# Loading v once per token and starting the first batch by other queues, in a chunked attention kernel with a ReGLU feed-forward

## The chip, the core and the metric

The kernel runs on one core of one Trainium2 chip. The engines that matter are TensorE (PE in the profile; PEld is its weight load), VectorE (DVE), ScalarE (ACT), GpSimd (POOL) and SyncE (SP). Transfers between HBM and SBUF are issued by POOL (queue q0 in the profile), SP (q1) or ACT (q10) and all run on the core's 16 DMA engines. The metric is the time of one execution in device microseconds. Three runs of the kernel before gave 247.49, 248.11 and 249.26 us; the median is 248.11.

## What is computed

Four batches, eight heads, 768 tokens, head size 64. Each chunk of 32 queries attends to 8 memory keys of its head, 16 keys to the left of the chunk, its own 32 and 8 to the right: 64 keys in all, fewer at the two ends of the sequence. The result, with the heads side by side, is a 3072 x 512 matrix that goes through a gated feed-forward of width 1536.

```python
for c in range(nc):                                  # chunk = 32, left 16, right 8
    k_full = concatenate([mem_k, k[:, :, l_start:r_end]], axis=2)
    v_full = concatenate([mem_v, v[:, :, l_start:r_end]], axis=2)
    scores = scale * matmul(q_c, k_full.T)
    a = exp(scores - max(scores)); a = a / (sum(a) + 1e-09)
    out[:, :, chunk c] = matmul(a, v_full)
x = out.transpose(0, 2, 1, 3).reshape(B * S, H * D)
result = (maximum(x @ w_gate, 0) * (x @ w_val)) @ w_out
```

All inputs and the result are float32 in HBM. The kernel computes in 16-bit types and accumulates in float32.

## The kernel before

**Tiles and blocks.** A tile is 128 tokens of one batch (four chunks, all eight heads). There are 24 tiles, six to a batch, numbered through. The feed-forward works on blocks of two or four tiles (`BLOCKS = [2, 2, 2, 4, 4, 4, 4, 2]`), so blocks 0 and 1 are tiles 0 to 3.

**One tile's attention.** q and k are brought to a layout with the head dimension on partitions (TensorE transposes, L225 for the first batch, L264 later, DMA transposes for the last six tiles). `scores` (L298) makes the 128 x 512 scores of a tile in 32 small matmuls. Then a chain over VectorE and ScalarE: row maximum (L311), subtraction (L318), exponential in three pieces (L326), row sum (L330), reciprocal (L334), normalisation (L341). `p_t` transposes the probabilities (L347), a copy takes them to SBUF, `values` multiplies them with v, and a copy gives the tile's columns of `xT`, the feed-forward's input.

**v in slots.** From batch 1 on, v lies in `v_bd`, two buffers used in turn. For every pair of heads and every chunk, the buffer holds a block of 128 partitions by 128 columns: 64 rows for the first head's keys in the left 64 columns, 64 for the second head's in the right 64, zeros elsewhere. Rows 0 to 55 of each half are the 56 tokens of the chunk's context, rows 56 to 63 the memory values. Since neighbouring chunks overlap, one load of 56 rows per chunk (`load_v_rows`, L173, two per batch: one for each half) brings most tokens twice. The zeros are written by POOL (L129), the memory values are copied into all 24 chunks of a pair of heads by eight small transfers per batch (`mem_rows`, L156; 8 partitions by 24 pieces of 128 bytes each), by SP for batch 1 and by POOL for batches 2 and 3. With this layout one matmul per chunk and pair of heads gives the tile's values (L377, 16 per tile).

**v in the first batch.** Here v is loaded tile by tile as it lies in HBM (`load_v_tile`, six transfers), and TensorE shifts it into chunk windows by multiplying with slices of a band matrix (`shift`, L204, 68 matmuls in all), with a copy by ScalarE or VectorE behind each of twelve groups. `values` then needs four matmuls for the memory values (L363) and 32 half-height ones for the rest (L370) per tile.

**q and k in the first batch.** They are loaded by POOL in three pairs of tiles (L216; k and q, 256 KB each in SBUF, converted to bfloat16 on the way) and transposed in 96 small TensorE transposes (L225).

**Feed-forward.** `first` (L396) multiplies the block's `xT` with 128 columns of `w_gate` or `w_val` at a time, four matmuls for each; ScalarE takes the rectified gate out (L402), VectorE multiplies it with the other half (L408). `second` (L421) multiplies with `w_out`, ScalarE takes the result out and stores it. The weights are loaded by POOL in four groups of columns (`load_gate_val`, L109), and blocks 0 and 1 are worked off in turn, group by group, since the weights are still on their way.

**What sets the order.** The kernel lists all operations with durations that it assumes, what they depend on, and priorities. `schedule()` runs through assumed time and picks, for each engine, the first ready operation; the result is a fixed order of instructions on each engine. On the chip each engine follows this order, and an instruction whose inputs are late holds up everything behind it on its engine. POOL's order (the loads) is written out by hand. [...]

Of the kernel before, what the change touches and what calls it, by code (L numbers as in the profile page):

```python
# [19 lines left out]
def kernel(  # L20
# [12 lines left out]
    nc = tc.nc  # L33
# [19 lines left out]
    BAND0 = 48  # L53

    LATE_QK, LATE_P = 18, 18

# [25 lines left out]

    band = const.tile([128, BAND0 + 176], F16, name="band")
    ident_h = band[:, BAND0:BAND0 + 128]
# [12 lines left out]
    v_q = v_bd[0][:, 0:2].rearrange("p h c d -> p (h c d)").rearrange("p (h c d) -> p h c d", h=HP, d=D)  # L97
    v_n = {}
    qk_p = {(i, r): const.tile([128, H, 2 * D], BF16, name=f"qk_p_{i}_{r}") for i in range(2) for r in range(TPB // 2)}
# [15 lines left out]
    def make_band():  # L115
        nc.gpsimd.memset(band, 0.0)
        nc.gpsimd.affine_select(
            out=band, in_=band, compare_op=ALU.not_equal, fill=1.0, base=BAND0,
            pattern=[[-1, BAND0 + 176]], channel_multiplier=1)
# [8 lines left out]
    def zero(eng, t, hp):  # L128
        eng.memset(t[:, hp].rearrange("p c d -> p (c d)").bitcast(F32), 0.0)  # L129


    def mem_load():
        for par in range(2):
            nc.sync.dma_start(
                kmem_f[:, par, :],
                bass.AP(tensor=mem_k.tensor, offset=mem_k[0, par, 0, 0].offset,
                        ap=[[2 * NMEM * D, B * HP], [D, NMEM], [1, D]]),
            )
# [13 lines left out]
    def mem_rows(eng, b, n):  # L152
        hp, par = divmod(n, 2)
        p = slice(64 * par + CTX, 64 * par + CTX + NMEM)
        src = vmem[p, b, HP * par + hp]
        eng.dma_start(  # L156
            v_bd[b % NSET][p, hp, :, D * par:D * par + D],
            bass.AP(tensor=src.tensor, offset=src.offset,
                    ap=[src.ap[0], [0, NCH], [1, D]]))
# [18 lines left out]
    def v_parts(b, par, c0, c1):  # L178
        parts = []
        if (b, par, c1) == (B - 1, 1, HP * NCH):  # L180
            c1 -= 1
            parts.append((b, par, 0, 48, c1, c1 + 1))
        return parts + [(b, par, 0, CTX, c0, c1)]


    def load_v_tile(t):
        v_n[t] = ldpool.tile([128, H, D], F16, tag="qk_b", name="v_n")
        nc.gpsimd.dma_start(
            v_n[t],
            bass.AP(tensor=v.tensor, offset=v[0, 0, 128 * t, 0].offset,  # L190
                    ap=[[D, 128], [S * D, H], [1, D]]))

    def shift(c0):
        ps = TMP["sh", c0] = fps.tile([128, 2, HP, D], F32, tag="fps", name="vs_ps")
        for i in range(2):
            t, g = divmod(c0 + i, 4)
            parts = [(t, BAND0 + CH * g - 16)]
            if g == 0 and t:
                parts.append((t - 1, BAND0 + 112))
            if g == 3 and t < TPB - 1:  # L200
                parts.append((t + 1, BAND0 - 48))
            for n, (src, x) in enumerate(parts):
                for par in range(2):
                    nc.tensor.matmul(ps[D * par:D * par + D, i], lhsT=band[:, x:x + 64],  # L204
                                     rhs=v_n[src][:, HP * par:HP * par + HP, :],
                                     start=(n == 0), stop=(n == len(parts) - 1))

    def shift_copy(c0, eng):
        copy(eng, v_q[:, :, c0:c0 + 2, :].rearrange("p h c d -> p c h d"), TMP.pop(("sh", c0)))

# [37 lines left out]
    def new_batch(b):  # L248
        qT[b] = kvpool.tile([128, HP, S], BF16, name="qT")
        kT[b] = kvpool.tile([128, HP, NCH, KW], BF16, name="kT")  # L250
        src = kmemT[:, b]
        nc.vector.tensor_copy(
            kT[b][:, :, :, 16:16 + NMEM],
            bass.AP(tensor=src.tensor, offset=src.offset,
                    ap=[src.ap[0], [NMEM, HP], [0, NCH], [1, NMEM]]))
# [101 lines left out]
    def values(a):  # L357
# [3 lines left out]
        if b == 0:  # L361
            for hp in range(HP):
                nc.tensor.matmul(ps[:, hp, :], lhsT=vmem_0[:, hp, :], rhs=x[:, hp, :],  # L363
                                 start=(hp == 0), stop=False, skip_group_check=True)
            for hp in range(HP):
                for g in range(4):
                    r = slice(CH * g, CH * g + CH)
                    for par in range(2):
                        p = D * par
                        nc.tensor.matmul(ps[p:p + D, hp, r], lhsT=v_q[p:p + CTX, hp, 4 * t + g, :],  # L370
                                         rhs=x[p:p + CTX, hp, r], start=False, stop=(hp, g) == (HP - 1, 3),
                                         skip_group_check=True)
            return
# [83 lines left out]
    op("warm", {"DVE": 0.15}, lambda e: nc.vector.memset(warm, 0.0), prio=(-9,))  # L457
    op("warm2", {"ACT": 1.5}, lambda e: nc.scalar.activation(warm, warm, ACT.Exp), ["warm"], prio=(-9,))
    op("vmem_f", {"DVE": 0.55}, lambda e: nc.vector.memset(vmem_f, 0.0), prio=(-8,), after=["warm"])
    op("kml", {"SP": 1.4}, lambda e: mem_load(), prio=(-9,))  # L460
    op("vml", {"SP": 1.4}, lambda e: pattern_load(), ["vmem_f"], prio=(-8,), after=["kml"])
    op("if", {"DVE": 0.25}, lambda e: nc.vector.tensor_copy(ident_f, ident_h), ["ident"], prio=(-7,))
    op("ib", {"DVE": 0.25}, lambda e: nc.vector.tensor_copy(ident_b, ident_h), ["ident"], prio=(-6.9,))
    op("kmt", {"PE": 0.25}, lambda e: mem_keys_t(), [("kml", 1.8), "if"], prio=(-5,), take=["aps"])
    op("kmc", {"ACT": 0.35}, lambda e: nc.scalar.copy(kmemT.rearrange("p b h m -> p (b h m)"), TMP.pop("kmem")),
       ["kmt"], prio=(-5,), give=["aps"])
    op("vm0", {"DVE": 0.5}, lambda e: nc.vector.tensor_copy(vmem_0, vmem_f), [("vml", 1.8)], prio=(-3,))
    for b in range(B):
        op(("new", b), {"DVE": 0.4}, lambda e, b=b: new_batch(b), ["kmc"], take=["kv"],
           prio=(-4.5,) if b == 0 else (1, TPB * b - 2, 0), after=[("t", TPB * b - 2, 0)] if b else [])  # L470
# [31 lines left out]
    for a in range(NT):  # L502
        b, t = divmod(a, TPB)
        last = t == TPB - 1
        for i in (1, 0):
            if b == 0:
# [7 lines left out]
            if a >= LATE_QK:  # L514
# [8 lines left out]
               (1, a - i, 0), ["aps"], ["qk"], pace(max(a - i, 0)))  # L523
            op(("tc", a, i), psum16(HP * 128), lambda e, a=a, i=i: qk_copy(a, i, engine[e]), [("t", a, i)],
               (1, a - i, 0), (), ["aps"])
        op(("s", a), {"PE": 0.36}, lambda e, a=a: scores(a),
           [(("t", a, 0), LAND) if a >= LATE_QK else ("tc", a, 0), ("tc", a, 1)]
           + ([] if last else [("tc", a + 1, 1)] if b or t % 2 == 0 else [("tc", a + 1, 1), ("tc", a + 2, 1)])
           + ([("tc", a ^ 1, 0)] if b == 0 else []), (1, a, 1), ["sps"],
# [14 lines left out]
        if b == 0:  # L544
            for c0 in (4 * t, 4 * t + 2):
                need = {c // 4 for c in (c0, c0 + 1)} | {max(c0 - 1, 0) // 4, min(c0 + 2, NCH - 1) // 4}
                gone = ([t - 1] if c0 % 4 == 0 and t else []) + ([t] if c0 == NCH - 2 else [])
                op(("sh", c0), {"PE": 0.4}, lambda e, c0=c0: shift(c0), [("vn", n) for n in sorted(need)] + ["ident"],
                   (1, a, 7.5), ["fps"], ["qk"] * len(gone), [("s", t)])
                op(("shc", c0), psum(2 * HP * D), lambda e, c0=c0: shift_copy(c0, engine[e]), [("sh", c0)],  # L550
                   (1, a, 7.6), (), ["fps"])
        blk = block_of[a]
        j = a - starts[blk]
        op(("v", a), {"PE": 0.45 if b else 1.0}, lambda e, a=a: values(a),
# [64 lines left out]
    for t in range(3):  # L619
        load_v_nat(t)  # L620
# [170 lines left out]
```

## Time and profile before

| | |
|---|---|
| three runs, median | 248.11 us (247.49 to 249.26) |
| the profiled execution, its own time | 247.81 us |
| its span, first to last instruction | 246.0 us |
| PE busy | 233.3 us, 95% |
| DVE, ACT, POOL busy | 132.7, 117.6, 90.6 us |
| PE busy in 0 to 15, 15 to 20, 20 to 25 us | 7.37, 3.84, 4.89 us |
| first feed-forward matmul | 22.24 us |
| queue q0 (POOL) | 94368 packets, 16.42 MB |
| queue q1 (SP) | 11760 packets, 2.64 MB |

Busy times are sums over instructions on an engine. PE's busy time says that matmuls were under way, not that they ran at their best rate, so the start-to-start distance of groups in the timeline is used for prices. Times within the span count from its start. The time of an execution is 1.8 us longer than its span.

### The profile page before, as it was taken

What the parts mean: (1) busy time and instruction counts of PE and PEld (TensorE: products, weight loads), DVE (VectorE), ACT (ScalarE), POOL (GpSimd) and SP (SyncE); (2) the same over time, 40 slices, a digit from 0 to 9 for tenths busy, and PEclk for the clock granted to TensorE, in tenths of its full rate; (3) what the DMA queues carried; (4) which work ended last, traced back from release to release, by engine and by line L of the source; (5) the groups of instructions that cost most, each with busy time, mean ns of one, the idle gap of its engine ahead of it and who ended that gap; (6) DMA issues with size and microseconds to landing.
All of it is one profiled execution on the core that took longest, in us unless ns stands there. A gap on an engine that the chain in (4) does not pass through costs nothing.

```text
span 246.0 us, 6397 instructions
## 1 busy us (share of the span) xinstructions
PE 233.3 (95%) x2673; PEld 139.8 (57%) x2673; DVE 132.7 (54%) x260; ACT 117.6 (48%) x265; POOL 90.6 (37%) x105
## 2 busy tenths in 40 slices
PE   0869999999999999999999999999999999999994
PEld 0646887884488645555445545555445444444873
DVE  2372757984139748796048779999342034320430
ACT  2755867753275445643245575765332232312432
POOL 8965799813268991099921050000000000000000
PEclk9999999999999999999999999999999999999999
DMA  7999999999999899999999999671101210002102
GB/s 74 173 179 203 203 96 119 174 175 127 133 223 154 80 102 136 75 75 147 179 192 158 67 76 109 130 147 25 23 0 45 85 44 0 0 35 95 43 3 85
DMA packets 109757, 25.76 MB, mean 105 GB/s; under 512 B 100769, under 2 KB 106657, under 8 KB 109729
## 3 DMA queue, kind: packets, MB, share of 16 engines
q0 software_dynamic: 94368, 16.42, 107.7%
q1 hardware_dynamic: 11760, 2.64, 8.9%
q10 hardware_dynamic: 3600, 6.29, 7.9%
q8 instruction: 21, 0.34, 0.6%
q14 instruction: 8, 0.06, 0.1%
HBM read 32.06 MB, written 6.29 MB: 156 GB/s over the span
## 4 chain that ended last, share of the span: by engine, by line
PE 92%; DMA 2%; DVE 2%; issue 1%; ACT 1%; POOL 1%; ACTq 0%; POOLq 0%
PE v_ps L396 26%; PE g_ps L396 26%; PE out_ps L421 25%; PE xT_ps L377 3%; PE s_ps L298 3%; PE qk_ps L264 2%; DMA qk_p<-in_k_dram 2%; PE pT_ps L347 2%; PE xT_ps L370 2%; PE vs_ps L204 1%; PE qk_ps L225 1%; PE xT_ps L363 1%; DVE mx L311 1%; POOL qk_p L216 1%; DVE dif L318 1%
## 5 line engine op out<-in xcount | busy, mean ns | idle before, releaser
L408 DVE TENSOR_TENSOR gvT<-v_ps,g_relu 128x256 f16<-128x256 f32 (+1 forms) x96 | 53.0, 555 | 56.7 <-PE v_ps L396 41.0
L396 PE MATMUL g_ps<-xT,w_gate_sb 128*128 128x256 f16 (+1 forms) x384 | 78.5, 327 | 0.0
L396 PE MATMUL v_ps<-xT,w_val_sb 128*128 128x256 f16 (+1 forms) x384 | 78.2, 326 | 0.0
L402 ACT ACTIVATE g_relu<-g_ps 128x256 f16<-128x256 f32 (+1 forms) x96 | 46.9, 489 | 50.7 <-PE g_ps L396 50.0
L421 PE MATMUL out_ps<-w_out_sb,gvT 128*128 128x512 f16 (+2 forms) x300 | 65.7, 371 | 0.0
L396 PEld LDWEIGHTS <-w_gate_sb 128*128 128x128 f16 x384 | 36.4, 98 | 24.0 <-issue 0.4
L396 PEld LDWEIGHTS <-w_val_sb 128*128 128x128 f16 x384 | 35.9, 98 | 20.9 <-issue 0.2
L421 PEld LDWEIGHTS <-gvT 128*128 128x128 f16 x300 | 28.0, 98 | 29.9
L78 ACT COPY o_sb<-out_ps 128x512 f32<-128x512 f32 (+2 forms) x25 | 14.2, 567 | 37.2 <-PE out_ps L421 28.2
L326 ACT ACTIVATE p_exp<-dif 128x256 f16<-128x256 f32 (+2 forms) x72 | 19.5, 336 | 9.0 <-DVE dif L318 8.8
L243 POOL DMA_DIRECT2D qk_b<-in_k_dram x18 | 16.5, 915 | 15.0 <-issue 8.4
L311 DVE TENSOR_REDUCE mx<-s_ps 128x8 f32<-128x512 f32 x24 | 16.5, 688 | 8.3 <-PE s_ps L298 8.0
L156 POOL DMA_DIRECT2D v_bd<-vmem x16 | 10.1, 642 | 27.7 <-DMA v_bd<-in_v_dram 27.7
L330 DVE TENSOR_REDUCE sm<-p_exp 128x8 f32<-128x512 f16 x24 | 16.4, 682 | 6.0 <-ACT p_exp L326 5.9
L78 ACT CAST xT<-xT_ps 128x512 f16<-128x512 f32 x19 | 11.1, 584 | 15.4 <-PE xT_ps L377 10.2
L243 POOL DMA_DIRECT2D qk_b<-in_q_dram x18 | 16.4, 913 | 3.1 <-issue 2.0
L341 DVE TENSOR_TENSOR p_n<-p_exp,rinv 128x512 f16<-128x512 f16 x24 | 16.5, 687 | 0.4
L318 DVE TENSOR_TENSOR dif<-s_ps,mx 128x512 f32<-128x512 f32 x24 | 16.4, 684 | 0.4
L173 POOL DMA_DIRECT2D v_bd<-in_v_dram x7 | 14.0, 2015 | 1.0 <-POOL v_bd L129 0.6
L377 PEld LDWEIGHTS <-v_bd 128*128 128x128 f16 x288 | 9.6, 96 | 4.7 <-issue 1.1
L78 ACT COPY kT<-qk_ps 128x512 bf16<-128x512 bf16 x17 | 10.8, 641 | 2.9 <-PE qk_ps L225 1.9
L129 POOL MEMSET v_bd<- 128x1536 f32 x8 | 10.7, 1397 | 0.0
(52 smaller groups left out, 156.8 us busy)
## 6 DMA issues: line engine op xcount, KB each, us to landing
out_dram<-o_sb ACTq DMA_DIRECT2D x23, 256.0 KB
v_bd<-in_v_dram POOLq DMA_DIRECT2D x5, 672.0 KB, 17.6
qk_b<-in_k_dram POOLq DMA_DIRECT2D x18, 128.0 KB, 6.1
qk_b<-in_q_dram POOLq DMA_DIRECT2D x18, 128.0 KB, 6.4
w_out_sb<-in_moe_w_out_dram POOLq DMA_DIRECT2D x2, 768.0 KB, 11.2
qk_p<-in_k_dram POOLq DMA_DIRECT2D x3, 256.0 KB, 5.2
qk_p<-in_q_dram POOLq DMA_DIRECT2D x3, 256.0 KB, 7.1
v_n<-in_v_dram POOLq DMA_DIRECT2D x6, 128.0 KB, 6.5
```

Of the source, the lines that this page charges most:

```text
L78: nc.scalar.copy(o, i)
L243: nc.gpsimd.dma_start(qk_b[a, i], bass.AP(tensor=x.tensor, offset=x[b, 0, 128 * t, 0].offset, ap=[[D, 128], [S * D, H], [1, D]]))
L311: nc.vector.reduce_max(SM[a, "mx"], s4, axis=AX.X)
L318: nc.vector.tensor_tensor(out=SM[a, "dif"].rearrange("p (m r) a s -> p r m a s", r=2), in0=S_ps.pop(a).rearrange("p r (m a) s -> p r m a s ...
L326: nc.scalar.activation(p[:, :, :, s0:s0 + k1 - k0], dif[:, :, :, k0:k1], ACT.Exp, scale=SCALE)
L330: nc.vector.reduce_sum(SM[a, "sm"], SM[a, "p"], axis=AX.X)
L341: nc.vector.tensor_tensor(out=P_n[a], in0=SM.pop((a, "p")), in1=rinv_b, op=ALU.mult)
L377: nc.tensor.matmul(ps[:, hp, r], lhsT=v_bd[b % NSET][:, hp, 4 * t + g, :], rhs=x[:, hp, r], start=True, stop=True)
L396: nc.tensor.matmul(ps, lhsT=w[:, f, 128 * m:128 * m + 128], rhs=xTs[blk][:, f, :], start=(f == 0), stop=(f == NFC - 1))
L402: nc.scalar.activation(st["r", m], st.pop((0, m)), ACT.Relu)
L408: nc.vector.tensor_tensor(out=st["gv"][:, m, :], in0=st.pop((1, m)), in1=st.pop(("r", m)), op=ALU.mult)
L421: nc.tensor.matmul(st["o", t, c], lhsT=st["gv"][:, m, 128 * t:128 * t + 128], rhs=w_out_sb[:, m, c[0]:c[1]], start=(m == 0), stop=(m == ND ...
```

## The change

Six things change together.

1. **v once per token.** `load_v_rows` now loads only 32 rows per chunk (rows 0 to 31 of a slot: 16 tokens left of the chunk and its first 16). Rows 32 to 55 are the same tokens as rows 0 to 23 of the next chunk's slot, and VectorE copies them there within SBUF (`upper`, eight copies per batch). A tail of 16 rows comes by a small load of its own (`ve`).
2. **The first batch in the same slots.** `shift`, its copies, the band matrix and the L363/L370 matmuls go; `values` uses the 16 matmuls of L377 for all tiles. v of batch 0 is loaded by two 32-row loads (a 16-row piece of them apart) right behind the identity. The zeros of its buffer are written by VectorE and ScalarE in twelve pieces (`zero_other`), the copies of tiles 0 and 1 come apart (`upper_tile`), and the memory values of batch 0 are brought into the slots by eight `mem_rows` transfers issued by SP.
3. **q and k of tiles 0 and 1** are loaded as float32 into a part of `v_bd[1]` by SP (k) and ACT (q), one transfer of 128 partitions by 8 pieces of 256 bytes per tile, and converted by ScalarE or VectorE (`raw_cast`). Three small SP loads (`next_load`) bring the eight keys to the right of tiles 0, 1 and 3. Tiles 2 to 5 keep the paired loads.
4. **Idle products.** While TensorE has nothing to do before the planner's 14 us, 153 products of a zeroed 128 x 128 tile are put into its order.
5. **The order of loads** on POOL is another: identity, v of batch 0, weight group 0, pair 1, weight group 1, and so on; the zeroing of `v_bd[1]` stands between weight groups. `v_bd[0]` needs no second zeroing.
6. **The planner** lets an engine wait up to 0.4 us for a more urgent operation in its first 24 us, no longer assumes slower TensorE work at the start, and has other priorities for the first tiles.

The core of the diff:

```diff
-    def load_v_tile(t): ...
-    def shift(c0): ...
-    def shift_copy(c0, eng): ...
+    def upper(b, par, i0, i1, eng):
+        x = v_bd[b % NSET].rearrange("p h c d -> p (h c) d")
+        d = slice(D * par, D * par + D)
+        copy(eng, x[64 * par + CH:64 * par + CTX, i0:i1, d], x[64 * par:64 * par + CTX - CH, i0 + 1:i1 + 1, d])
+    def idle_product(N):
+        if "idle" not in TMP:
+            TMP["idle"] = fps.tile([128, 512], F32, tag="fps", name="idle_ps")
+        nc.tensor.matmul(TMP["idle"][:, 0:N], lhsT=idle, rhs=idle[:, 0:N], start=True, stop=True)
+    def raw_load(eng, x, a, i):
+        src = (q, k)[i]
+        n = 128 if a < HEAD else NMEM
+        eng.dma_start(qk_f[0:n, x], bass.AP(tensor=src.tensor, offset=src[0, 0, 128 * a, 0].offset,
+                    ap=[[D, n], [S * D, H], [1, D]]))
+    def raw_cast(x, a, i, eng):
+        qk_b[a, i] = ldpool.tile([128, H, D], BF16, tag="qk_b", name="qk_b")
+        copy(eng, qk_b[a, i], qk_f[:, x])
...
     def mem_rows(eng, b, n):
-        src = vmem[p, b, HP * par + hp]
+        src = vmem[p, b, HP * par + hp] if b else vmem_0[p, hp, D * par:D * par + D]
...
     def values(a):
-        if b == 0:
...
-            return
         for hp in range(HP):
             for g in range(4):
                 nc.tensor.matmul(ps[:, hp, r], lhsT=v_bd[b % NSET][:, hp, 4 * t + g, :], rhs=x[:, hp, r], ...)
...
+    for n in range(2 * HP):
+        op(("mr", 0, n), {"SP": 0.72}, lambda e, n=n: mem_rows(nc.sync, 0, n), ["vm0"], (0, 0))
...
         op(("v", a), {"PE": 0.45}, lambda e, a=a: values(a),
-           ... ([("vl", b, 0, n) for n in range(2)] if b else [("shc", 4 * t), ("shc", 4 * t + 2), "vm0"])
-           + ([("mr", b, n) for n in range(2 * HP)] if b else []), ...
+           ... [("mr", b, n) for n in range(2 * HP)] + [("z0", t, par) for par in range(2) if b == 0]
+           + ([("up", b, n) for n in range(2 * HP)] + ... if a >= HEAD else [("up0", a, par) for par in range(2)]), ...
...
+    load("ident", 0, 0, make_ident)
+    load_v_op(0, 0, [])
+    load_v_op(0, 1, [])
+    load_w_op(0)
+    load_pair_op(1, 1)
+    load_pair_op(1, 0)
+    load_w_op(1)
...
```

`vm0`, on which batch 0's `mem_rows` depend, is VectorE's conversion of memory values that SP loads (`pattern_load`); in SP's order that load stands behind k of tile 0, half of the memory keys and the three small key loads, and k of tile 1 stands between it and the eight `mem_rows`.

## The prediction

> **What bounds the kernel now.** I read the page first (slices, chain), then the chain in order of time and the timeline of the first 45 us.
>
> ```profile
> span 246.0 us, 6397 instructions
> ...
> PE   0869999999999999999999999999999999999994
> ...
> PE 92%; DMA 2%; DVE 2%; issue 1%; ACT 1%; POOL 1%; ACTq 0%; POOLq 0%
> ```
>
> After the first three slices TensorE is never free, and the chain is 92% TensorE. So two things set the time: the work left on TensorE once its stream is dense, and when that is. The chain in order of time, first 32 us:
>
> ```profile
> 3.84 5.23 DMA qk_p<-in_k_dram
> ...
> 16.62 0.59 PE xT_ps L363 x4
> ...
> 21.04 0.59 ACT xT L78
> ...
> 22.31 0.97 PE g_ps L396 x4
> ...
> 25.68 0.44 PE g_ps L396 x4
> ```
>
> The start waits for k, then tile 0's values begin at 16.62, tile 1's columns are out at 21.63, and the feed-forward begins at 22.3. Its first group of four takes 0.97 us, one at 25.68 takes 0.44: eight of L225's transposes take 0.64 us until 21.7 and 0.39 at 24.75. TensorE runs at about half speed until then, although the page's clock row shows 9 throughout. Everything before 22.3 that is not late costs nothing; every microsecond by which the feed-forward starts later is paid in full.
>
> **Work that goes, behind 22.3 us.** The timeline of TensorE:
>
> ```profile
> 26.73 0.85 PE L204 MATMUL vs_ps<-v_n,band 128*64 128x256 f16 x12
> 27.50 0.61 PE L396 MATMUL g_ps<-xT,w_gate_sb 128*128 128x256 f16 x4
> ...
> 31.23 0.39 PE L363 MATMUL xT_ps<-pT,vmem 128*128 128x128 f16 x4
> 31.55 0.68 PE L370 MATMUL xT_ps<-pT,v_bd 56*64 56x32 f16 x32
> 32.16 0.61 PE L396 MATMUL g_ps<-xT,w_gate_sb 128*128 128x256 f16 x4
> ```
>
> Start to start, twelve shift matmuls hold TensorE 27.50 - 26.73 = 0.77 us, one tile's old values 32.16 - 31.23 = 0.93. The new form is L377's, 1.06 us for two tiles in the chain, 0.53 each. Behind 22.3 stand 46 of the 68 shift matmuls (at 23.55, 26.73, 40.02 and 42.77: 1.3 + 0.77 + 0.77 + 0.67 = 3.5 us) and the values of tiles 2 to 5 (4 x 0.40 = 1.6). **-5.1 us**, certain. The others of both kinds lie in a start with 9 us of idle TensorE.
>
> **When the feed-forward starts.** q and k of tile 0 come first and alone, v right behind: tile 0's probabilities can be there by about 14 (q and k at 5 by their 0.5 MB at the 173 to 203 GB/s of the first slices from 2.1 us on, then 9 us as from 6.20 to 15.3 before). [...] SP's rows in the timeline:
>
> ```profile
> 2.10 0.85 SPq L165 DMA_DIRECT2D v_bd<-in_mem_v_dram  x2
> 37.15 6.52 SPq L156 DMA_DIRECT2D v_bd<-vmem  x8
> ```
>
> and queue q1 in the DMA view for 37 to 44 us, then for 44 to 54:
>
> ```profile
> q1 hardware_dynamic: 776, 0.10, 13.5%
> ```
>
> ```profile
> q1 hardware_dynamic: 824, 0.10, 13.4%
> ```
>
> Eight transfers of 192 packets, each with a closing packet for each of its eight partitions, are 1600 packets; 776 + 824 = 1600, and the view for 54 to 60 has no q1 line. So issuing took 6.5 us, moving until 54: **16.8 us from the first issue**. In the first window POOL's queue carries 128-byte packets of q and k, in the second w_out in pieces of 1 KB, and the small packets take turns with them.
>
> [...] Memory values: issued at 5 or a little later; before, they were issued at 2.10 and VectorE's conversion began at 6.40, 4.3 us later, so conversion at 9.4, 0.43 long, first row issued at 9.9. From there: with nothing in the way 6.5 us of issue and some 2 us to land, 18.4, or 15.5 if the memory values land as soon as 7; with all of it at 82 packets per us, as in the second window, 1600/82 = 19.5, or 29.4. In 10 to 24 us POOL's queue is never empty: v until about 12, then 512-byte pieces of weights, 256-byte pieces of pair 1, and from 17 or so the 1 KB pieces of weight group 1. That is the mix of before with less of the slowest, so of 16.8 I take 14: **values(0) at 24**, against 16.62.
>
> Behind it nothing moves. TensorE's next entries are pair 1's transposes, tile 1's probabilities and its values. On ScalarE, tile 0's xT copy stands before tile 1's exponential, so tile 1's chain hangs on values(0) too. From values(0) to the first gate group: values 1.06 (slow clock, twice 0.53), xT 0.58, exponential 0.81, sum 0.68, reciprocal 0.20, normalise 0.69, transpose 0.61, copy 0.58, values 1.06, xT 0.58 = 6.85, and 0.3 of handoffs (0.02 to 0.05 each in the chain): 31.15, against 22.3, **+8.9**. Eight transposes of pair 2 stood ahead of 22.3 (in the sixteen at 20.92) and now stand behind: **+0.3**. TensorE has waited some 9 us for values(0) and then has sparse work, so I take it as slow when the feed-forward comes, as it was at 22.3 after waits of 1.4 to 4.2 us; before, 0.6 us of feed-forward and scores were lost to that behind 22.3 (0.97 for 0.44, 0.34 for 0.25), now about 2.5 us at half speed, 1.2: **+0.6**. Tile 2's scores stand behind the first gate group and its transposed probabilities only eight groups (3.5 us) later, while its chain needs 3.9 plus five gate products of 0.42 in between: **+0.3**, partly hidden by the slow groups. Sum: -5.1 + 8.9 + 0.3 + 0.6 + 0.3 = +5.0. The profiled execution took 247.81 (246.0 and 1.8 around), 0.3 below the median: **252.8**.
>
> [...] The page shows no slow clock, the durations do: 0.97 against 0.44, with TensorE over three quarters busy from 15 us on. [...]
>
> **Parts at nothing.** The idle products end before values(0) by their place, in time that TensorE has free; each is at most one 128-column matmul late. Weights come no later: ahead of group 1 stood five paired loads and five v tiles, now four float32 tiles, all of v and two pairs; with weight group 0 that is 5.0 MB in HBM before and 4.7 now. Group 1 was first used at 27.5. The 36 copies of v are new on VectorE, with no row of their kind: between 0.29 us per 512 elements (kT<-k_t) and 0.68 (L408 from PSUM), 24 of 1536 and 12 of 1024 elements are 28 to 65 us by the rows' full price, which holds their fixed part several times; I take 0.4 us a copy, 14 us, since k_t's is cut into pieces of 16. VectorE is 54% busy, and the copies stand in 60 to 140 us, where it has 6 to 10 us free in 20. If not, gate products wait and TensorE behind four PSUM buffers. The new copies also wait for v in VectorE's order; v's load falls from 10752 to 6176 packets a batch, and for batch 2 no longer waits for 5.35 us of zeroing by POOL, so it should be there; if not, rival 3.
>
> **Rivals.**
> 1. *Rows quick (faster).* values(0) at 16 if the conversion comes at 7 and the rows move as fast as they are issued. For it: early on the packets beside are small, and 37 to 44 us, with small ones, moved half. Against: even then 776 packets took 7 us. Then the chain of 6.3 us (fast clock) gives 22.3, the slow 0.6 us goes as well: 247.81 - 5.1 + 0.3 - 0.6 = 242.4. It decides from values(0) before about 18.
> 2. *Even.* values(0) at 18 to 20: the feed-forward 3 to 5 us later, against 5.1 and the small terms: 246.8 to 248.8.
> 3. *Copies held up (slower still).* v of batch 2 or 3 lands late, as it did at 104.8 and about 140 before (POOL waited for it 9.2 us at most), and now the copies stand before gate products on VectorE: up to 4 us each, 254 to 260.
> 4. *The early start is hidden anyway:* values(0) comes at 16, and the feed-forward, after group 0's 1.8 us (four groups of 0.44), waits for group 1 until 27.5. That gives back 3 of the 5.1: about 246. Against: before, nothing waited for it.
>
> [...]
>
> **How the numbers follow.** Forecast (values(0) at 20 to 28, 248.8 to 256.8): 0.50; rival 1: 0.28; rivals 2 and 4: 0.14; rival 3: 0.08. Faster by over 1% (about what a measurement can tell here) has rival 1, 0.28, and a little of 2: 0.30. Within 1%: most of 2 and 4, 0.13. Slower: 0.57. The range reaches from rival 1's 242 to the forecast's end and the nearer half of rival 3, 242 to 257.5; the forecast's own is 248.8 to 256.8.
>
> **What would show it.** Right: TensorE's longest wait in the first 30 us is for DMA v_bd<-vmem, the first L377 at 20 to 28, the first L396 some 7 us later, group of four at 0.9 us or more at first, L204 gone. Wrong: first L377 before 18, or long VectorE waits for in_v_dram behind 40 us.

## The result, and the profile after

The changed kernel takes 260.17 us in the median (259.14 to 262.67, four runs), the kernel before 248.45 (247.49 to 249.26, four runs beside it): ratio 1.049, 95% interval 1.040 to 1.057. It is slower by some 12 us. Here and below, runs more than 1.5% above the fastest of their kernel are left out of medians and ratios, which concerns `rows_split` and `rs_quiet` alone. The profiled execution took 260.17 us with a span of 258.4, against 247.81 and 246.0 before.

First the page of the changed kernel: span, TensorE's busy tenths in 40 slices of 6.46 us, the granted clock in the same slices, and the chain by engine.

```profile
span 258.4 us, 6394 instructions
...
PE   5865399999969999899999999999999999999994
...
PEclk9979569999999999999999999999999999999999
...
PE 75%; DVE 10%; DMA 8%; SPq 2%; issue 2%; ACT 2%; ACTq 0%; DVEq 0%
```

Before, TensorE was dense from the fourth slice on and made up 92% of the chain. Now the fifth slice has a 3 (the start is later), and there is a 6 at 71 to 78 us and an 8 at 103 to 110, which were not there. DVE, 2% of the chain before, has 10%. So there are two losses, one ahead of the feed-forward and one behind it. The line numbers are other ones now: values is L389 (L377 before), the feed-forward's first products L408 (L396), the transposes of the probabilities L372 (L347), the transposes of the pairs L246 (L225), `mem_rows` L200 (L156); the copies of v go through the helper at L80.

The first loss in the chain in order of time (start, duration, what), up to 35 us:

```profile
5.75 4.95 DMA v_bd<-in_mem_v_dram
...
11.28 0.84 SPq L200
...
17.42 10.29 DMA v_bd<-vmem
...
27.84 0.28 PE xT_ps L389 x4
...
34.05 0.97 PE g_ps L408 x4
```

The memory values land at 10.70, VectorE converts them at 10.83, SP issues the row transfers from 11.28 to 17.4, and the last one lands at 27.71. The last four matmuls of values(0) wait for it until 27.84; the other twelve began at 22.33. The feed-forward starts at 34.0 instead of 22.2.

The second loss, from the same view for 30 to 130 us:

```profile
66.74 3.25 DVE v_bd L80 x4
70.02 0.69 DVE sm L355
...
72.06 3.52 DVE v_bd L80 x4
75.59 0.70 DVE p_n L366
76.34 0.40 PE pT_ps L372 x4
```

Batch 1's eight copies of v stand on VectorE inside the softmax chain of tile 6: four ahead of the row sum, four ahead of the normalisation. TensorE has nothing left at 74.2 and waits. The chain of waits for 60 to 120 us (who, for whom, total us, times, longest):

```profile
PE pT_ps L372 <- DVE p_n L366: 3.4, 2, 2.2
```

The second of these two waits, 1.2 us at 108.6, lies behind batch 2's eight copies in the same way.

What the change was to bring is there too. The shift matmuls (L204) are gone, and v's loads land sooner: on the page's list of transfers (count, size, median us from issue to landing) the first line is of before, the second of after.

```profile
v_bd<-in_v_dram POOLq DMA_DIRECT2D x5, 672.0 KB, 17.6
```

```profile
v_bd<-in_v_dram POOLq DMA_DIRECT2D x7, 384.0 KB, 10.2
```

**Accounts.** From the first gate group to the end the kernel before takes 246.0 - 22.2 = 223.8 us, the changed one 258.4 - 34.0 = 224.4. With the 4 to 5 us of work removed, that stretch should have been some 219.5; so about 11.8 us are lost ahead of 34.0 and about 5 behind it, against 4.5 won.

### The profile page after: what moved, and what is told of

It reads as the page before. It is cut to its first block, busy times and chain, and to the rows that moved or that the text cites. A ratio compares the mean times of both kernels' runs of the same rounds, so it can differ in the third digit from the quotient of the medians.

```text
span 258.4 us, 6394 instructions
## 1 busy us (share of the span) xinstructions
PE 237.3 (92%) x2626; PEld 145.2 (56%) x2626; DVE 158.6 (61%) x308; ACT 117.9 (46%) x265; POOL 80.9 (31%) x103
## 3 DMA queue, kind: packets, MB, share of 16 engines
HBM read 28.60 MB, written 6.29 MB: 135 GB/s over the span
## 4 chain that ended last, share of the span: by engine, by line
PE 75%; DVE 10%; DMA 8%; SPq 2%; issue 2%; ACT 2%; ACTq 0%; DVEq 0%
PE g_ps L408 23%; PE v_ps L408 22%; PE out_ps L433 21%; DVE v_bd L80 4%; DMA v_bd<-vmem 4%; PE xT_ps L389 3%; SPq L200 2%; PE s_ps L323 2%; DMA v_bd<-in_mem_v_dram 2%; PE pT_ps L372 2%; PE qk_ps L289 2%; DMA v_bd<-in_q_dram 2%; DVE gvT L420 1%; DVE p_n L366 1%; DVE mx L336 1%
## 5 line engine op out<-in xcount | busy, mean ns | idle before, releaser
L408 PE MATMUL g_ps<-xT,w_gate_sb 128*128 128x256 f16 (+1 forms) x384 | 78.9, 329 | 0.0
L408 PE MATMUL v_ps<-xT,w_val_sb 128*128 128x256 f16 (+1 forms) x384 | 78.7, 328 | 0.0
L408 PEld LDWEIGHTS <-w_gate_sb 128*128 128x128 f16 x384 | 36.6, 99 | 23.7 <-DMA w_gate_sb<-in_moe_w_gate_dram 0.2
L408 PEld LDWEIGHTS <-w_val_sb 128*128 128x128 f16 x384 | 36.0, 98 | 21.2
L433 PEld LDWEIGHTS <-gvT 128*128 128x128 f16 x300 | 28.0, 98 | 30.1
L80 DVE COPY v_bd<-v_bd 24x1536 f16<-24x1536 f16 (+3 forms) x36 | 24.0, 709 | 0.5
L217 POOL DMA_DIRECT2D v_bd<-in_v_dram x17 | 16.1, 1005 | 9.8 <-DMA w_out_sb<-in_moe_w_out_dram 5.1
L389 PE MATMUL xT_ps<-pT,v_bd 128*128 128x32 f16 x384 | 13.7, 177 | 4.9 <-DMA v_bd<-vmem 4.3
L389 PEld LDWEIGHTS <-v_bd 128*128 128x128 f16 x384 | 13.2, 96 | 8.9 <-issue 4.7
L149 PE MATMUL idle_ps<-idle 128*128 128x128 bf16 x153 | 14.3, 266 | 1.0 <-DVE idle L472 1.0
L78 ACT CAST xT<-xT_ps 128x512 f16<-128x512 f32 x18 | 10.5, 581 | 9.8 <-PE xT_ps L389 8.9
```

The costliest lines, as they stand in the source:

```text
L78: nc.scalar.copy(o, i)
L80: eng.tensor_copy(o, i)
L389: nc.tensor.matmul(ps[:, hp, r], lhsT=v_bd[b % NSET][:, hp, 4 * t + g, :], rhs=x[:, hp, r], start=True, stop=True)
L408: nc.tensor.matmul(ps, lhsT=w[:, f, 128 * m:128 * m + 128], rhs=xTs[blk][:, f, :], start=(f == 0), stop=(f == NFC - 1))
L433: nc.tensor.matmul(st["o", t, c], lhsT=st["gv"][:, m, 128 * t:128 * t + 128], rhs=w_out_sb[:, m, c[0]:c[1]], start=(m == 0), stop=(m == ND ...
```

## The experiments

All times are medians of the executions; the kernel before was run beside each group and took 248.16, 248.16, 247.81 and 248.16 us.

### The copies for batches 1 to 3 undone (`full_v`)

```diff
 def load_v_op(b, par, deps):
+    if b:
+        ...
+        load(("vl", b, par), CTX * n, ..., lambda: load_v_rows(b, par, 0, CTX, 0, last), deps)
+        return
...
-for b in range(B):
+for b in range(1):
     for n in range(2 * HP):
         op(("up", b, n), ...)
```

> Batches 1 to 3 load v twice per token, 56 rows of slots, as the kernel before; their 24 copies on VectorE are not issued; batch 0 as changed. Theory 'copies' (the copies stand in VectorE's order ahead of the softmax of the next batch's tiles, and TensorE runs out of work at 74 and at 108.6): the two waits of 2.2 and 1.2 us for p_n go, 0.7 comes back as in the kernel before, where values(6) waits for the longer load at 67.5; 260.2 - 3.4 + 0.7 = 257.5 us (256 to 258.2). Rival 'late v' (the later loss comes of loads pushed back by the late start, and v's longer loads make it worse): TensorE's waits stay at 3 us or more behind 60, for DMA v_bd<-in_v_dram: 259.5 to 263. The first gate group stays at 34.

Measured: 255.31 us (254.68 to 256.68), ratio to before 1.030 (1.025 to 1.035); the changed kernel's is 1.049. So 4.9 us are given back by undoing what was meant to be a gain, more than the 2.7 expected; the time lies below the expected 256 to 258.2. The page's TensorE row:

```profile
PE   5865299999999999999999999999999999999994
```

The 6 and the 8 have gone. In gaps over 0.05 us TensorE waits 0.5 us in all behind its first gate group (34.6), against 3.9 in the changed kernel. From there to the end this kernel takes 219.3 us, 4.5 less than the kernel before: the gain of fewer TensorE instructions, laid bare. That is 5.1 less than the changed kernel's 224.4. Gaps are 3.4 of it, as the theory said; where the other 1.7 went was not traced. Theory "copies" holds, and late v is refuted.

### One part alone, on the kernel before (`before_copies`)

```diff
 # before.py, batches 1 to 3 only
-load_v_rows(b, par, 0, CTX, c0, c1)
+load_v_rows(b, par, 0, CH, 0, c1)          # and 16 rows of the last chunk apart
+op(("up", b, n), {"DVE": ...}, upper(...), [("vl", b, 0, par)], (1, TPB * b - 1, 12))
```

> The kernel before, start and batch 0 untouched, with one part of the change alone: batches 1 to 3 load v once per token and copy the upper slots on VectorE, eight copies per batch ahead of its first values. Theory 'copies' (they cost by their place in VectorE's order, whatever the start): the wait for v at 67 us (0.7) goes, waits of 2.2 and 1.2 us for p_n come in the first tiles of batches 1 and 2: 248.2 + 3.4 - 0.7 = 250.9 us (249.8 to 252.5). Rival 'late start only' (the copies cost only because the late start pushed everything together): 247.3 to 248.7.

Measured: 250.21 us (249.59 to 250.72), ratio 1.008 (1.005 to 1.011). The copies cost 2.05 us net on a kernel whose start is untouched, inside the expected range and less than the 4.9 in the changed one. The wait for v at 67 us is gone as expected. Batch 1's copies found free time at 57 to 59 and 64 to 67.5; only batch 2's stand in a chain (TensorE's waits for 60 to 120 us):

```profile
PE pT_ps L352 <- DVE p_n L346: 1.2, 1, 1.2
PE s_ps L303 <- ACT qT L78: 0.7, 1, 0.7
```

So the part loses by itself. What it loses was not the same in the two kernels, and neither was the place that the planner gave the copies.

### The copies tile by tile (`tile_copies`)

```diff
-op(("up", b, n), ...)                     # eight copies of 24 x 1536 per batch
+op(("up0", a, par), {"DVE": 0.34}, upper_tile(par, a % TPB, ..., a // TPB), [("vl", a // TPB, par)], (1, a, 1.5))
```

> Batches 1 to 3 copy the upper slots tile by tile (two copies of 24 x 1024 ahead of each tile's softmax, three for the last tile) instead of eight copies of 24 x 1536 per batch ahead of the batch's first values; the loads of v are as changed. Theory 'place' (eight copies, 3.3 and 3.5 us, stand in one chain with the softmax of the batch's first tile; TensorE runs out of work behind them): the waits of 2.2 us at 74 and 1.2 at 108.6 shrink to under 0.8 together, 257.5 us (256.3 to 258.5). Rival 'total' (VectorE has no room for 14 to 19 us more at any place): waits move to the other tiles and stay over 2.5 us; 259.5 to 261.5.

Measured: 259.82 us (259.27 to 261.72), ratio 1.048 (1.042 to 1.053): no gain. TensorE's timeline at 75 us:

```profile
74.93 0.72 PE L398 MATMUL xT_ps<-pT,v_bd 128*128 128x32 f16 x16 [2.26 <-DVE pT L80]
```

The wait has moved one step on: four copies of v (1.67 and 1.28 us) and another tile's subtraction now stand between tile 6's normalisation and VectorE's copy of its transposed probabilities. Smaller pieces did not help, since the planner's order put them into the same chain. The time lies where the rival "total" had it, but not for its reason: between 80 and 100 us VectorE was busy only 12.4 us in 20 in the changed kernel.

### The batch-0 rows cut in two (`rows_split`)

```diff
-op(("mr", 0, n), {"SP": 0.72}, lambda e, n=n: mem_rows(nc.sync, 0, n), ["vm0"], (0, 0))
+op(("mh", n), {"SP": 0.72}, lambda e, n=n: mem_rows(nc.sync, 0, n, 0, 4 * HEAD), ["vm0"], (0, -1))
+op(("mr", 0, n), {"SP": 0.72}, lambda e, n=n: mem_rows(nc.sync, 0, n, 4 * HEAD, NCH), ["vm0"], (0, 0))
```

> Batch 0's eight memory-row transfers are cut in two: eight for chunks 0 to 7 (tiles 0 and 1) first, eight for chunks 8 to 23 behind them; values(0) and values(1) need only the first eight. Theory 'rows' (the landing of the rows sets values(0) and with it the feed-forward): the first eight are 576 packets instead of 1600; issued from 11.3 to 17.4 as before, at the 98 packets per us of the changed kernel's rows (1600 from 11.3 to 27.7) they land by 18 to 20, values(0) then goes by the probabilities at 22.2, and the first gate group at 34.0 - 27.8 + 22.9 = 29.1; 255.3 us (254.5 to 256.5). Rival 'k1' (the start is late anyway, since k of tile 1 lands at 14.7 and the exponential of tile 0 stands behind its conversion on ScalarE): values(0) comes at 22.3, but the first gate group stays at 32 or later; 258 to 260.5. Rival 'position' (the rows are late by the queue beside them, not by their number): the first eight land behind 25, less than 2.5 us gained.

Measured: 258.31 us (257.21 to 260.30, three runs), ratio 1.042 (1.036 to 1.049), which overlaps the changed kernel's 1.040 to 1.057 and misses the 254.5 to 256.5 of theory "rows". The profiled execution took 261.08 us, so it serves for the order of events and not for the time. The rows did come sooner, if not by the expected 20: the first eight, issued from 11.69 to 17.85, were there at 23.5, and values(0) ended at 23.8 instead of 28.1. But the first gate group came at 31.2, not 29.1, and 1.5 us were lost right behind it. The timeline shows the next holder:

```profile
21.80 4.97 DVE L80 COPY v_bd<-v_bd 24x1024 f16<-24x1024 f16 x5
23.23 1.40 POOL L129 MEMSET v_bd<- 128x1536 f32 x1
...
29.12 3.78 DVE L80 COPY v_bd<-v_bd 24x1024 f16<-24x1024 f16 x4
30.45 1.43 POOL L129 MEMSET v_bd<- 128x1536 f32 x1
...
33.71 0.41 PE L323 MATMUL s_ps<-kT,qT 64*32 64x64 bf16 x32 [1.50 <-DVE qT L80]
```

Tile 1's exponential is done at 25.3, but its sum stands on VectorE behind five copies that take 4.97 us; then four more stand ahead of tile 2's q. The same five copies took 4.93 us in the changed kernel, where the wait for the rows hid them, and 1.93 in `full_v`, where by chance no memset of POOL fell beside them.

### No batch-0 rows ahead of the values (`old_values0`)

```diff
 def values(a):
+    if b == 0:
+        ... # 4 products with vmem_0, then 32 of 56 x 64 with lhsT=v_bd[0][p:p + CTX, hp, 4 * t + g, p:p + D]
+        return
...
-    op(("mr", 0, n), ...)
```

> Batch 0's values take the memory as the kernel before does it, by four products with the memory values' own tile and 32 products of 56 x 64 with the slots of v; the eight memory-row transfers of batch 0 are not issued; everything else as changed. Theory 'rows': values(0) at 22.3 as the probabilities come, 1.5 us long at the slow clock instead of 1.06; the first gate group 5.9 us behind its end, and 0.45 for the longer values(1): 30.1, 3.9 earlier; four tiles behind it cost 0.40 each more: 260.2 - 3.9 + 1.6 = 257.9 us (257 to 259). Rival 'k1': the first gate group stays at 32 or later, 259.5 to 262.

Measured: 259.76 us (258.71 to 261.85), ratio 1.048 (1.042 to 1.054). values(0) was done at 22.3, 5.8 us earlier, and yet the first gate group came at 34.5: three copies took 5.21 us (21.38 to 26.59) ahead of tile 1's sum, two more 2.51 ahead of a copy of k that TensorE waited 2.7 us for. Taking away the wait that was last gave nothing that can be told from noise, because the copies were nearly as late. The figures are those of the rival (32 or later, 259.5 to 262), but its reason, k of tile 1, is not what stood last here.

### POOL's memsets moved, and taken away

`rs_quiet` is `rows_split` with POOL's four memsets of the second slots behind the early loads:

```diff
-load_zero(0) ... load_zero(3)             # between the weight groups
+for hp in range(HP):                      # ahead of batch 1's v
+    load_zero(hp)
```

> rows_split, and POOL's four memsets of the second slots (1.4 us each, at 16 to 31 us) are moved behind the early loads, ahead of batch 1's v. Theory 'POOL holds the copies' (a copy of v on VectorE, 0.41 us alone, waits while POOL's memset or DMA issue runs): the five copies ahead of tile 1's sum take 2.1 us instead of 4.97, the sum comes at 25.3 instead of 26.8, the next four take under 2 us instead of 3.78 and TensorE's wait of 1.5 us at 32.2 goes; first gate group at 29.7, 256.3 us (255.3 to 258). Rival 'slow by themselves' (the copies are as slow without the memsets): copies at 0.7 or more in the mean, first gate group at 30.7 or later, 258.5 to 260.5.

Its four runs took 253.13, 258.86, 260.83 and 261.59 us, too far apart for a ratio. In the profiled one (260.83) the five copies took 2.0 us and the first gate group came at 30.1, as theory "POOL holds the copies" has it. Why one run came out at 253 was not traced; a kT copy that began ahead of the memsets would do it, but that is not shown. In the profiled run this stands in the timeline at 42 us:

```profile
42.06 6.29 DVE L277 COPY kT<-kmemT 128x768 bf16<-128x768 bf16 x1
...
42.73 5.40 POOL L129 MEMSET v_bd<- 128x1536 f32 x4
```

A copy of batch 1's memory keys, with the four memsets beside it, took 6.29 us, and TensorE waited 4.5 for what stood behind it. In the kernel before both are there, but apart in time:

```profile
29.06 5.35 POOL L129 MEMSET v_bd<- 128x1536 f32 x4
...
37.44 0.35 DVE L252 COPY kT<-kmemT 128x768 bf16<-128x768 bf16 x1
```

The same copy takes 0.35 us alone. `rs_noz` has no memsets on POOL at all:

```diff
+op(("zz", hp, par), {"DVE": 0.8, "ACT": 0.85}, zero_second(hp, par, ...), [...], prio=(1, TPB - 2, 0), after=[("nrm", 2)])
-load_zero(hp)
```

> rows_split without POOL's four memsets: only the halves of the second slots that neither v nor rows fill are zeroed, in eight pieces of 64 x 768 by VectorE and ScalarE at 35 to 55 us, where both have free time. Theory 'POOL holds VectorE's copies between SBUF tiles': the nine copies ahead of the feed-forward take 0.41 to 0.6 us each (9 in under 5.5 instead of 8.75 in rows_split), kT<-kmemT takes under 1 us (6.3 behind four memsets in rs_quiet), the first gate group comes at 29.5 to 30.3 and the late waits of 2.0 and 1.2 us at 74 and 109 stay, since there it is DMA issues that stand beside the copies: 253.2 us (252 to 255), the time of the one run of rs_quiet that stood apart. Rival 'memsets are innocent': copies at 0.8 or more, 257.5 or more.

Measured: 256.79 us (255.80 to 257.51), ratio 1.037 (1.034 to 1.040); that is 1.5 us below `rows_split`, with intervals that overlap, so here the copies decide and not the time. The nine copies ahead of the feed-forward:

```profile
21.27 1.89 DVE L81 COPY v_bd<-v_bd 24x1024 f16<-24x1024 f16 x5
...
27.40 1.57 DVE L81 COPY v_bd<-v_bd 24x1024 f16<-24x1024 f16 x4
```

3.46 us instead of 8.75, and the first gate group at 29.45: theory right on both. The time is 3.6 above the 253.2 expected. The eight zeroing pieces on VectorE and ScalarE stand ahead of q and k copies, and TensorE waits 2.1 us for these at 40 to 44.5; that hiding place was not free. The late wait of 2.0 us at 69.7 stays.

### Tile 1's k earlier (`rs_k1`)

```diff
-prio=((-12, -12, -7, -10)[x],)            # k0, q0, k1, q1
+prio=((-12, -12, -11.5, -11.5)[x],)
```

> rows_split, and SP issues tile 1's k as its second transfer instead of its last before the rows. Theory 'rows and copies set the start': tile 1's k lands by 10 instead of 14.7, ScalarE's wait of 3 to 4 us for it goes and tile 0's probabilities are transposed at 18 instead of 21, but the memory values are issued up to 0.7 us later, values(0) still ends at 23.5 to 24.5 by the rows, and the first gate group stays at 30.5 to 32: 259 us (258 to 260). Rival 'k1': first gate group before 29.5, 257.5 or less.

Measured, on top of `rows_split`: 258.13 us (257.70 to 258.48), ratio 1.039 (1.035 to 1.044): no difference from `rows_split` (258.31) that these runs can tell. In the profiled runs tile 0's probabilities were transposed at 19.8 instead of 21.0, the rows were issued 2 us later (13.69), values(0) ended at 24.9 and the first gate group came at 30.3. But VectorE had the probabilities normalised at 19.74, against 19.87 in `rows_split`. Moving k forward moved the memory keys back (TensorE waited for them until 9.99 instead of 6.28), tile 0's scores came at 14.03 instead of 12.43, and zeroing pieces on ScalarE took the place of k's conversion. The transposes came sooner because the idle products ahead of them ended at 19.4 instead of 21.2. So this run does not show k of tile 1 to be a holder.

### The idle products left out (`no_idle`)

```diff
-order.append((t, lambda: idle_product(128)))
```

> The idle products are left out; the order of all else is as changed. Theory (they cost and bring nothing, since the wait until 27.8 loses the clock again): the first transposes and scores run slow, tile 0's probabilities come up to 1 us later and stay ahead of the rows; first gate group at 34 +- 0.5, its groups of four at 0.97 to 1.04 as now; 260.2 us (259.3 to 261). Rival (the clock that they raise is worth something): 261.5 us or more.

Measured: 261.18 us (260.42 to 261.39), ratio 1.052 (1.049 to 1.055), which overlaps the changed kernel's and lies between the theory's 261 and the rival's 261.5. The first gate group came at 33.0 in the profiled run, and at the slow pace, 1.04 us for the first, as with the products. In time they neither cost nor bring anything that these runs can tell. But they did hold something up. Tile 0's probabilities were expected up to 1 us later without them and were transposed 1.6 us earlier, at 19.56, right behind their normalisation. With the products (changed kernel, TensorE's timeline) the normalisation ends at 19.60, and TensorE, which works in order, first has these to finish:

```profile
17.61 3.72 PE L149 MATMUL idle_ps<-idle 128*128 128x128 bf16 x43
21.16 0.39 PE L372 MATMUL pT_ps<-ident_h,p_n 128*128 128x128 f16 x4
```

The granted clock had dropped to 0.50 in 18 to 20 us, behind a wait of 3.7 us, so 43 products took 3.72 us; in `old_values0`, at full clock, they took 2.58 and held nothing up. In the changed kernel the wait for the rows hides the 1.6 us.

### Putting the pieces together

`best` undoes the copies of batches 1 to 3, takes tiles 0 and 1's memory by products as before, and moves tile 1's k, POOL's memsets and the copies of tiles 2 to 5 (`full_v`, the old values for tiles 0 and 1, and the edits of `rs_k1` and `rs_quiet`):

```diff
 def values(a):
+    if a < HEAD:
+        ... # 4 products with vmem_0, then 32 of 56 x 64, as above
+        return
...
+op(("up", 0, n), ..., after=[("nrm", HEAD - 1)])
```

> Four things together: tiles 0 and 1 take the memory by products with its own tile as before (the rows are still moved, for tiles 2 to 5), tile 1's k is issued second on SP, POOL's memsets stand behind the early loads, the copies of tiles 2 to 5 behind tile 1's softmax, and batches 1 to 3 load 56 rows with no copies. Theory (start set by rows, copies and k1 in turn; later loss by copies): tile 0's probabilities at 18, first gate group at 25.5, 219.3 behind it as in full_v and 1.8 around: 246.6 us (245 to 249), at or under the kernel before. Rival (the start has another holder): first gate group at 28 or later, 249.5 us or more.

Measured: 258.00 us (257.06 to 258.21), ratio 1.038 (1.034 to 1.043), where 245 to 249 was expected. The first gate group came at 26.4, but the kT copy beside four memsets took 6.55 us here and cost TensorE 5.4; behind that wait the granted clock was down again (0.58 in 46 to 50 us). The other 6 us of the miss were not taken apart. `best2` has `rs_noz`'s zeros instead, and more idle products:

```diff
+op(("zz", hp, par), ...)
-HASTE, WARM = 24.0, 14.0
+HASTE, WARM = 24.0, 17.0
```

> best with the zeros of rs_noz instead of POOL's memsets, and idle products in the gaps up to tile 1's values. Theory: the wait of 5.4 us at 42.9 (gate products and a kT copy behind POOL's memsets on VectorE) goes, 258.0 - 5.4 = 252.6; the idle products keep the clock up over tile 1's values and the first six gate groups, which ran at half speed for 6.6 us in best, up to 3 us: 250.5 us (248.5 to 252.6). Rival (it beats the kernel before): 248 or less. Rival (another stall takes its place): 254 or more.

Measured: 251.62 us (251.42 to 251.87), ratio 1.016 (1.014 to 1.017): 8.5 us below the changed kernel, inside the expected range, with 26.6 for the first gate group. It is still 3.8 us above the kernel before, which starts at 22.2. Behind its first gate group it takes 223.3 us, 4.0 more than `full_v`: TensorE has gaps of 2.0 us in all there, up to 43.5 us, and its first six groups run at the slow pace. So the gain of fewer TensorE instructions is spent again. `best3` moves four more places of the order and extends the idle products:

```diff
-prio=((-12, -12, -11.5, -11.5)[x],)
+prio=((-12, -12, -10, -10)[x],)           # behind the memory keys at -11
+op("vm0", ..., after=[("sub", 0)])
+op(("up0", a, par), ..., after=[("sub", a)])
+op(("up", 0, n), ..., after=[("max", HEAD)])
-HASTE, WARM = 24.0, 17.0
+HASTE, WARM = 24.0, 20.0
```

> best2 with four places of the order changed: tile 1's q and k behind the memory keys on their queues, VectorE's conversion of the memory values and the copies of tiles 0 and 1 behind tile 0's and 1's subtraction, the copies of tiles 2 to 5 behind tile 2's maximum, and idle products in the gaps up to tile 1's values. Theory: tile 0's scores at 10.5 instead of 13.9, as their keys no longer stand behind the memory values, first gate group at 23.2 instead of 26.6; VectorE's 0.7 us in front of tile 2's q goes: 251.6 - 3.4 - 0.7 = 247.5 us (245.5 to 249.5), about the kernel before. Rival (weights or v now hold the start): 250 or more.

Measured: 254.05 us (252.97 to 255.85, six runs), ratio 1.024 (1.021 to 1.028), where 245.5 to 249.5 was expected. Tile 0's scores came only at 12.4, tile 1's values at 26.0 behind the transposes of the second pair, and TensorE stood for 2.0 us at 28.2 on nothing that the profile names. The added idle products were in the way too: tile 0's normalisation ended at 17.6, its transposes came at 18.6 behind fifteen of them. What the 2.0 us were, and whether this way of starting can reach 22 us at all, stays open. No version here beats the kernel before.

## Why the prediction was right and wrong

The prediction said slower (0.57) at 252.8 us; the time is 260.2, beyond the range's 257.5. Term by term:

- **Work that goes, -5.1: right to some 0.6 us.** From the first gate group to the end, `full_v` needs 4.5 us less than the kernel before; the prediction's terms for that stretch (-5.1, and the +0.3, +0.6 and +0.3 of pair 2, the slow clock and tile 2) come to -3.9.
- **values(0) waits for the rows: right mechanism, term too small.** By the kernel's list of dependencies values(0) needs all eight transfers, and the longest wait of TensorE ahead of 30 us, 4.3 us, is for `v_bd<-vmem`, as the signs asked for. That SP issues the memory values "at 5 or a little later" was my estimate, which no run had shown: their two loads went out at 5.43 and 5.75, behind a wait of SP of 1.9 us that the trace puts down to tile 0's q. The conversion came at 10.8 instead of 9.4, since the memory values took 5 us to land instead of 4.3 and were issued at 5.75; from first issue to last landing the rows took 27.71 - 11.28 = 16.4 us instead of 14, nearly the 16.8 of before. I had shortened that 16.8 for a lighter mix beside it, without a row that showed a lighter mix to be quicker. Together values(0) ends its wait at 27.8 instead of 24.
- **The chain to the feed-forward, 7.15: 6.2,** because twelve of values(0)'s sixteen matmuls ran ahead of the last rows. The first gate group came at 34.0 instead of 31.15: 2.8 us of the miss.
- **"Tile 0's probabilities can be there by about 14": wrong, and hidden.** They were transposed at 21.2. VectorE had tile 0's subtraction done at 13.9. k of tile 1, issued last, landed at 14.7; ScalarE, after a wait of 4.1 us, converted it, copied it and zeroed two pieces ahead of tile 0's exponential, which began at 17.1. The normalisation ended at 19.6, and then the idle products held the transposes for 1.6 us. I had followed q and k of tile 0 only. Which of these an edit would get back is open: `rs_k1` moved k and gained 0.1 us at the normalisation.
- **"Parts at nothing", the 36 copies: the step that failed.** I took 0.4 us a copy and 14 us in all, hidden because VectorE has 6 to 10 us free in 20. They took 24.0 us, as this line of the changed kernel's page has it (busy us, mean ns, idle us before):

```profile
L80 DVE COPY v_bd<-v_bd 24x1536 f16<-24x1536 f16 (+3 forms) x36 | 24.0, 709 | 0.5
```

The size was wrong, and so was the hiding, which was argued from an average: the copies stand inside the softmax chain of a batch's first tile, which TensorE waits for. Undoing those of batches 1 to 3 gives 4.9 us back (`full_v`, 255.3 us, inside the stated range). In sums: from the first gate group on, the prediction has 223.8 - 3.9 = 219.9 us and the changed kernel takes 224.4, 4.5 more; with the 2.8 ahead of it this is 7.3 of the 7.4 us by which 260.2 exceeds 252.8.

- **Rival 3 came nearest (254 to 260, at 0.08), with another reason,** late v ahead of gate products. v was not late: no long wait of VectorE for `in_v_dram` stands behind 40 us. The copies themselves were late.
- **Rivals 1, 2 and 4** needed values(0) before 20 and fell with it.
- **Weights at nothing: right** (0.2 us of waiting for them in the changed kernel).
- **Idle products at nothing: right in the time by luck.** "At most one 128-column matmul late" is wrong: 43 of them stood ahead of tile 0's transposes and held these for 1.6 us (`no_idle`), hidden only because the rows were later still.

Why a copy costs 0.4 us here and 2 there is in the traces copy by copy. Alone, 24 x 1024 elements take 0.41 us and 24 x 1536 take 0.55. With POOL's issues of q and k back to back beside them (66 to 70 us) the latter take 0.95; the one at 72.6, beside the issues of v's loads, took 1.90; a memset beside one makes up to 2.1. `rs_noz` shows it by taking the memsets away: 0.38 us a copy in the mean. Other work of VectorE beside memsets kept its times: the sum at 26.80 in `rows_split`, beside the memset at 26.54, took 0.69 us, and in the kernel before, beside the four memsets from 29.06 to 34.4, a subtraction took 0.68 and the gate products 0.41 and 0.42. So in these runs the memsets held up copies and not VectorE as a whole; why these, they do not tell.

On the clock, which the prediction took as slow when the feed-forward comes: in the changed kernel it was. The granted clock is 1.00 in 24 to 26 us, 0.50 in 28 to 36 and 1.00 again from 38; TensorE had been idle from 23.5 to 27.8. The first three groups (0.97, 0.97 and 0.85 us for 0.44) cost 1.5 us more than at full pace, near the 1.2 that I took. This stretch alone makes no rule: `best2`, below, shows a fall without such an idle stretch. The idle products did not make the first work fast either: four transposes took 0.63 us until 8.5 and 0.39 from 9.9.

## What to carry to other kernels

Removing the wait that ends last gives only the distance to the next one: here rows, copies of v and tile 0's late probabilities stood within a few microseconds of each other. The single edits of the start gave 0.4 to 1.9 us, none clear of the noise, where all together brought the first gate group from 34.0 to 26.6. The last 4.4 us to the 22.2 of before stay unexplained. Work that is "hidden" on a half-busy engine has to be placed in that engine's order, instruction by instruction, beside the chain that uses it; an average share of free time hides nothing. The same goes for filler: TensorE worked in order, and the idle products held up tile 0's transposes behind them by 1.6 us. And a copy between SBUF tiles on VectorE should be priced together with what POOL does at that moment: 24 x 1024 elements took 0.41 us alone and up to 2.1 beside a memset.

## What the runs showed of the hardware that I had not expected

- **A waiting VectorE copy did not get in between POOL's memsets.** The kT copy of 0.35 us waited through all four in `rs_quiet` (6.29 us, memsets 5.40) and in `best` (6.55, memsets 5.41).
- **POOL's DMA issue held such a copy up only in part.** In the changed kernel the copies at 99.11 and 105.76 ran at their own 0.55 us with an issue beside them, those at 67.3 to 69.0 took 0.95 and the one at 99.6 took 0.91.
- **The clock fell without an idle stretch.** In `best2` TensorE's longest gap between 20 and 26.5 us is 0.65 us, and its granted clock still went from 1.00 to 0.50. From 22.5 us on it had only transposes and the small products of tile 1's values to do; whether such work counts less for the clock than other work these runs do not tell. The columns of this view are: stretch, its length, busy us (and instructions) of PE, PEld, DVE, ACT and POOL, granted clock, DMA share, GB/s.

```profile
22.00:24.00 2.00, 1.35 (x31) 1.18 (x29) 1.86 (x5) 0.92 (x2) 1.52 (x2) 1.00 1.33 206
24.00:26.00 2.00, 1.67 (x54) 1.36 (x53) 1.95 (x5) 1.29 (x3) 0.60 (x2) 1.00 1.41 205
26.00:28.00 2.00, 1.24 (x12) 0.56 (x8) 1.91 (x5) 0.90 (x2) 1.24 (x3) 0.64 1.57 202
28.00:30.00 2.00, 1.68 (x39) 1.22 (x40) 1.15 (x3) 0.00 (x0) 0.94 (x2) 0.50 1.79 198
```

- **The clock row told of a fall, not of the first slow stretch.** Without the idle products it reads 1.00 in 34 to 36 us, while four gate matmuls take 1.04 there, as with 0.50 in the changed kernel. `before_copies`, whose start is that of the kernel before, shows both ends: its twelve shift products at 12.3 took 0.85 us (1.49 in the kernel before), so its clock had been up, and the row reads 0.50 in 16 to 24 us, where the kernel before has 1.00 at the same slow pace (means of the two profiled executions: 0.977 and 1.000).
